# A rewritten order of steps, and 40 unread matmuls in front, in a fused linear-attention and MLP kernel on one core

## The chip, the cores and the metric

One Trainium2 chip, of which the kernel uses one core. The metric is the device time of one execution in microseconds (us). Times are medians over runs. The profile is one further execution, taken by the hardware profiler; its span runs from the first instruction of the program to the last.

## What is computed

For 8 batches of 8 heads (576 tokens, 64 channels each) the reference computes linear attention with a learned feature map, puts the heads of a token side by side (512 channels, 4608 tokens in all), and sends each token through a two-layer network with an ELU between the layers:

```python
def phi(x):
    proj = np.einsum('bhsd,df->bhsf', x, w_phi)                 # 64 -> 128
    proj = proj - np.max(np.abs(proj), axis=-1, keepdims=True)
    return np.concatenate([np.exp(proj), np.exp(-proj)], axis=-1)
q_p, k_p = phi(q), phi(k)
kv  = np.einsum('bhsf,bhsd->bhfd', k_p, v)
num = np.einsum('bhsf,bhfd->bhsd', q_p, kv)
den = np.einsum('bhsf,bhf->bhs', q_p, np.sum(k_p, axis=2))[..., None] + 1e-06
x = (num / den)          # then (4608, 512), heads side by side
h = x @ w_in             # 512 -> 2048
g = np.where(h > 0, h, np.exp(np.minimum(h, 0)) - 1)
out = g @ w_out          # 2048 -> 512
```

All matmuls of the kernel are in bf16 with fp32 accumulation; the output is fp32.

## The kernel before, in words

**Two halves.** The attention half works on 16 groups n of four heads, two groups to a batch. The network half works on 9 chunks of 512 tokens; chunk b consists of tokens of batch b, and the ninth collects the last 64 tokens of each batch. Both halves run interleaved over the whole kernel, so that one half's matmuls fill the time in which the other's elementwise work is under way.

**An order written by hand.** The program is one string, `ORDER`, of 1797 letters. Every letter is one step of a fixed kind with its own list of arguments, and each time a letter occurs it takes the next argument of its list. A star chooses the other engine or form, a digit the PSUM bank that the step begins to fill. Instructions are emitted in the order of the string. Each engine runs its own instructions in that order and waits for the data of others through semaphores. So for each engine the string fixes what stands ahead of what, and nothing else does. PSUM has 8 banks; a step that fills a bank waits until the bank's previous content has been read.

The kinds of step that the prediction uses, with their lines:

- loads on GpSimd's queue: `e`, `f`, `g` (L209: keys, queries, values of a batch, converted to bf16), `h` (L218: the two halves of `w_in`), `i` (L221: `w_out`)
- transposes of keys and queries: for groups 0 to 3 on TensorE, `j`, `l` (L233), with their PSUM copies `k`, `m` (L240); for the other groups by a DMA, `n`, `o` (L254, L259) on SyncE's queue
- keys: `A` (L287, project), `C` (L305, VectorE takes the largest absolute value), `B` (L298, ScalarE takes both exponentials), `D` (L315, the exponential of the maxima), `E` and `F` (L324, L333, GpSimd scales the values), `U` (L509, 36 matmuls each, the key-value product), `V` (L519, its copy)
- queries: `M` (L346, L361), `N` (L374, L388, maxima on VectorE), `O`, `P`, `Q` (L414 to L426, the maxima are split and transposed), `S` (L469, L481), `T` (L493, exponentials on ScalarE), `W` (L542, L558, the product with the key-value matrix), then the division (`X` or `x`, `R`, `y`, L572 to L608), and the transposes of the result, `Y`, `Z` (L623, L633) or the DMA `z` (L649, L656)
- network: `p` (L665, four matmuls, of 512 columns, or of 256 in chunk 0), `q` (L676, exponential on ScalarE), `r` (L681, clamp on GpSimd), `s` (L685, ELU on VectorE), `t` (L693, four matmuls of 512 columns), `u` (L703, copy), `v` (L709, store)
- start: `a` (L174 to L179, the load of `w_phi`, three memsets on VectorE, the identity on GpSimd), `b` (L182, L187, bf16 copies of `w_phi`), `c`, `d` (L192, L201, selector matrices on VectorE)

TensorE works on the whole array (128 rows) in `p`, `t`, `W`, `P`, `Y`, `j`, `l`, and on the upper and the lower 64 rows in turn in `A`, `M`, `S`, `U`. There are 550 TensorE steps of 3914 matmuls in all, each with a weight load of its own.

Of the kernel before, what the change touches and what calls it, by code (L numbers as in the profile page):

```python
# [15 lines left out]


ORDER = """
eeeacj0j5dkk*bA6CA1A3CBBBBDj0kj5kA6CCBBfl0l2BBmmM1NOgDA4BBfl0l7gmm*P1QS2TCDefA0CTM6NOhhgiEEEFFU4
EEUDM2NV*W6XBBP2Q*S4TTM0NM2NFFEU6EEUOP1Qj0j3S4kkM1NV*W6Xl0S2mTTTTl1mY5Z*Y7j6kZOP0W3XQ*S0TTA5Cp2q  # L20
rp7qM3NrssS0TTBp4qA0p3p2CBqrrsj7kl6mqrssM4Np7p3BBM0Np6A4enfDFqrsqrqBrssCp2qp0Y7p3p1rqrZ*O*qrBW6E
sssDqFrl2m*P4Q*p0p5qrXqrEEssM2Np4qrES6TM0NsS2TTTM0NsY6Zp7qrO*sA0A2BBBU4UVCp7qrsp6qrsP5QBt4S0TCp7
qrsp5p6W2XzTW0XDp7EEFqrqrqttA0nS2TTssrsCBp5qrtu*p7p2p3p4t6qrgDBszsqp5qrqS0rstrTsoFsEqp4Tp7rqzS2s
A0rTtEsCToU4qA2BUrzstV*CBW4up7XW0qBt6rXzDBM4FtNzM0M2sA4NvBp7tNqBzrA0sM2O*BCftBENP7t5uQCEDS2M6TtN
FeTS0M6ETtNTEU2S0A6UTCop4VtqTp3rzBsW0qnp4Xrp2qszW0rqu*O*p3DXvBEp5qsvrp7qrszp6rqsFsA0rqM2np4NBEp5
qCrzP3p2rQ*sqp3srqsDp7rqsfp6sqrBp5rsqEsM0qA2p4NBrt7BrsqFS0CgtTsrTS2EM5TNS0toTsTA5U2CTUBS0VvtBW2z
Tt6XTW4uzA0DXS2BtETzCtFETtzBA2M4BS0t7oTCtDTNFtEBvM0A4EM2NBtzNeBU0fu*UA2Cp6Bp5Cqut4rDBsEp7qM2V*r
p6NqEDnW0wstwrqxgM2trNW0FnetxEp5vusS0qM2Rp7syTNp6TFrqS2Rp4qsrTrsp5qsTp7rqysW0qS2xp6rTzrTp4sEzsq
A0U2qCroUrsBp7RV*syA5BCW2p4zxDqW0Eqxp3Brp2rBsRqA0S5qCnt7rTgRtsvTrstBEvsDS3M5TytNzTt2yu*BW3EzS5x
A0tBFzTRM3CtyTNFtzBEwM5S0vU3NTUToA5Vt7BuA0CtCzDtBEW2BtfxBA4p6BRyp3CqDEW0u*wp2qxrBp7FqFsrS0M4TEt6  # L30
NTtrsqtRrsM0ysM3p5NEzp7qNp2rzqsW0rqp4nxrp5qevstrsqsrS0uU2RTUy*S6TzVp4TsW0vqp3xTrp5qoRrsA0qS6p2CT
rp4TsvqsW6qp3rzBrsp5qexBt2rqRS0DA6srotBsytBsyTA3CtETCzW5Dt7FxFBEtBnRM0yA5M3NBztEutNBzEM0wU2CvfUN
DS4V*Et6uW0TvW2xTtxA4M0BntRBW2Nyzp7ECtqt1xFDrup5FsEA2qM6p4NBrp0ECqU6srBUqM2V*tNrA5sS2Bp7swRp4TRC
yqp0TrztqsBtzrqgy*S2u*W5Torp7xDTp1sqS2qRvW5rsTp4rsTp0zyxqW2Fqp7zrsrsA5qvp1gRBxrp4qsBp3rsqyp2Cqrw
zt7sqrsS0EM5sTtnNTrtEDzsS0M3A5TEtCoTt2NFBEA0U3BCURM5Dty*BEVztBNEW3zu*A0S5xBtTt7CTW3RDtxBEA5wM0B
u*FS3ytNBEtTCp2TFuW0qU3xM5rURM0NV*p7yNp4zqsrS5qA0p3sTroCp2Tqsp7qrW4qrsp6DrsBnp3Rqsp2qrvxBt7rzqs
A0S4srBtsBp6y*TCzp3qRp2qrvwtrsqzsDtrTEsvM0A3M5NBp2ENp1qBru*p0qEsvt7qCFrM5p2rsW3NqtrstFsExA0S5Bty
TCt4TRW2By*txzDA0U5BRS2zUyBtEV*zCtuFDEvW0TS5xt7TEzTtu*ETS0U2TFS4UwTtVW0p6xp3qRTRW0rtqyTp2rxp5qs
p4rqRW0rsqp6sursp3yqsp7qrzxp5rqy*zp4qrssW0rzqt6Rrsp3zxp7qy*W0rsqp2xrp5qstrsqtRrsp4systqzRp7rzst5
qtrvsty*tzt7ztvttt4ttp3p2qp1rqstrqsp3rsp2qt1rqsp0rsp3qtrqsp2rsp0qu*p3rqvstrqsup6rvsp5qp3rqsp2rqs  # L40
p6rqstrqst5rsp3p6qp2rqstrqsp3rsp6qutrqvsp7rsp3qp6rqstrqsup7rvst4qutrvstup7vp6qtrqst5rsp7u*p6qvtr
qstrstt7p6p4qtrqsp3rstqtrsp6t4qutruvstvtt7utvttt6tutvtt7u*tvttuv
"""


# [1 line left out]
def kernel(  # L47
# [10 lines left out]
    nc = tc.nc  # L58
# [36 lines left out]
    psum = ctx.enter_context(  # L95
        tc.tile_pool(name="psum", bufs=1, space=bass.MemoryType.PSUM)
    ).tile([P, 8, 512], FP32, name="banks")
# [18 lines left out]
    mhl = [consts.tile([P, 2, D], BF16, name=f"mhl{j}") for j in range(2)]  # L116
# [24 lines left out]

    FIRST = 2
    PLACE_OF = (
        ((0, 1, 5, 6, 2, 3, 4, 7, 8), (0, 1, 4, 5, 2, 3, 6, 7, 8)),
# [189 lines left out]
    def m_mm(n, c, bank=None):  # L336
        if n >= JOINED:
# [32 lines left out]
    def m_max(n, c):  # L370
        if n >= JOINED:
# [357 lines left out]
    def blocks(name, n):  # L729
# [33 lines left out]
        O=(m_split, m_parts),  # L763
# [5 lines left out]
        x=(x_join, x_thirds), R=(x_rec, x_thirds), y=(x_scale, x_thirds),  # L769
# [45 lines left out]
```

## Time and profile before

| | |
|---|---|
| time, median of 3 runs (range) | 366.57 us (366.25 to 367.02) |
| span of the profiled execution | 366.1 us |
| TensorE busy | 347.7 us, 95% of the span |
| VectorE, ScalarE, GpSimd busy | 268.3, 252.5, 212.7 us (73, 69, 58%) |
| first matmul starts, last matmul ends | 4.50 us, about 361.6 us |
| chain that ended last, by engine | TensorE 80%, VectorE 8%, DMA 7%, ScalarE 2%, "issue" 2% |

"Issue" stands for time in which an engine waited for nothing that the profile shows. [...]matmuls overlap in the record: 512 columns have a mean of 380 ns, while a run of four starts one every 216 ns. A busy TensorE is therefore not the same as a TensorE at its peak, and times of steps are read from start to start. The page gives the granted TensorE clock as full in every one of its 40 slices.

### The profile page before, as it was taken

The numbers are of one execution on the slowest core, as the hardware profiler recorded it, in microseconds if no ns is written. First come the engines' busy times: TensorE is split into PE (matmuls) and PEld (weight loads), VectorE is DVE, ScalarE is ACT, GpSimd is POOL, SyncE is SP. The second block draws the span as 40 slices with busy tenths as digits, with TensorE's granted clock in tenths as the row PEclk, the third lists the DMA queues.
The fourth block names the chain that finished last, engine by engine and source line by source line (L and its number), as shares of the span: only waits on it lengthen the run. The fifth ranks groups of instructions, "written<-read, shape, count | busy, mean of one in ns | idle before, by whom it ended". The sixth has DMA issues, their size and how long they took to land.

```text
span 366.1 us, 9813 instructions
## 1 busy us (share of the span) xinstructions
PE 347.7 (95%) x3914; PEld 188.8 (52%) x3914; DVE 268.3 (73%) x474; ACT 252.5 (69%) x481; POOL 212.7 (58%) x323
## 2 busy tenths in 40 slices
PE   2897999999999999999999999999999999999995
PEld 1675676655465444545465445544555444444442
DVE  4887986878976889788979899899858814744300
ACT  4887887878897689876976886888577304554220
POOL 8852857277934878485786497456557504543200
PEclk9999999999999999999999999999999999999999
DMA  7999956699796999965988298053220330213143
GB/s 115 202 213 207 208 82 109 105 159 149 119 144 89 159 135 167 172 96 81 184 165 141 33 181 133 8 109 77 46 48 16 32 75 2 58 29 89 28 98 75
DMA packets 68478, 39.70 MB, mean 108 GB/s; under 512 B 48336, under 2 KB 62800, under 8 KB 68432
## 3 DMA queue, kind: packets, MB, share of 16 engines
q1 hardware_dynamic: 52416, 20.56, 33.3%
q0 software_dynamic: 15856, 18.35, 32.9%
q8 instruction: 30, 0.49, 0.5%
q10 hardware_dynamic: 160, 0.16, 0.1%
q14 instruction: 16, 0.13, 0.1%
HBM read 36.77 MB, written 9.44 MB: 126 GB/s over the span
## 4 chain that ended last, share of the span: by engine, by line
PE 80%; DVE 8%; DMA 7%; ACT 2%; issue 2%; POOL 1%; ACTq 0%; DVEq 0%; POOLq 0%
PE banks L693 32%; PE banks L665 29%; PE banks L509 5%; DMA kn<-in_k_dram 4%; DMA kT<-kn 3%; PE banks L542 3%; PE banks L469 3%; PE banks L287 3%; DVE mk L305 2%; PE banks L558 2%; DVE gT L685 2%; PE banks L346 2%; DVE mq L388 1%; PE banks L361 1%; ACT EK L298 1%
## 5 line engine op out<-in xcount | busy, mean ns | idle before, releaser
L681 POOL TENSOR_SCALAR e_sb<-e_sb 128x512 f32<-128x512 f32 (+1 forms) x160 | 90.9, 574 | 97.0 <-ACT e_sb L676 94.9
L693 PE MATMUL banks<-w_out_sb,gT 128*128 128x512 bf16 x576 | 138.2, 380 | 0.0
L685 DVE SCALAR_TENSOR_TENSOR gT<-e_sb,banks 128x512 bf16<-128x512 f32 (+1 forms) x160 | 96.7, 626 | 44.9 <-POOL e_sb L681 44.5
L676 ACT ACTIVATE e_sb<-banks 128x512 f32<-128x512 f32 (+1 forms) x160 | 87.6, 562 | 60.3 <-PE banks L665 56.9
L665 PE MATMUL banks<-xT,w_in_sb 128*128 128x512 bf16 (+1 forms) x576 | 122.9, 356 | 1.0 <-DVE mq L388 0.9
L665 PEld LDWEIGHTS <-w_in_sb 128*128 128x128 bf16 x640 | 58.8, 98 | 58.6 <-issue 2.7
L298 ACT ACTIVATE EK<-banks 128x768 bf16<-128x768 f32 x96 | 75.3, 814 | 14.6 <-PE banks L287 11.4
L693 PEld LDWEIGHTS <-gT 128*128 128x128 bf16 x576 | 52.5, 98 | 59.8 <-issue 1.9
L324 POOL TENSOR_TENSOR vs<-vn,em 128x576 bf16<-128x576 bf16 x64 | 73.5, 1159 | 15.8 <-ACT em L315 15.7
L493 ACT ACTIVATE Eq<-banks 128x768 bf16<-128x768 f32 (+2 forms) x96 | 73.3, 813 | 9.5 <-PE banks L481 6.1
L305 DVE TENSOR_REDUCE mk<-banks 128x6 f32<-128x768 f32 x48 | 45.3, 951 | 7.9 <-ACT EK L298 3.7
L374 DVE TENSOR_REDUCE mx<-banks 128x6 f32<-128x768 f32 (+1 forms) x30 | 30.7, 1038 | 4.8 <-PE banks L346 3.8
L608 POOL TENSOR_TENSOR xj<-xs,recj 128x448 bf16<-128x448 f32 (+1 forms) x22 | 20.1, 915 | 14.5 <-DVE recj L603 10.6
L703 ACT COPY o_sb<-banks 128x512 f32<-128x512 f32 x23 | 13.3, 590 | 14.5 <-PE banks L693 14.5
L587 DVE TENSOR_TENSOR xs<-banks,e 128x455 f32<-128x455 f32 (+1 forms) x30 | 18.1, 602 | 7.2 <-PE banks L542 5.8
L509 PE MATMUL banks<-vs,EK 64*128 64x65 bf16 x1152 | 23.2, 194 | 0.0
L509 PEld LDWEIGHTS <-EK 64*128 64x128 bf16 x1152 | 21.4, 97 | 2.3 <-issue 1.3
L542 PEld LDWEIGHTS <-Eq 128*128 128x128 bf16 x400 | 16.2, 97 | 7.3 <-issue 1.3
L592 DVE TENSOR_TENSOR xs<-banks,xs 128x455 f32<-128x455 f32 (+1 forms) x30 | 18.3, 609 | 1.1
L287 PE MATMUL banks<-w_sb,kT 64*128 64x128 bf16 x288 | 17.0, 229 | 1.3 <-DMA kT<-kn 0.6
L542 PE MATMUL banks<-kv_sb,Eq 128*128 128x65 bf16 x400 | 17.3, 194 | 0.5 <-DVE kv_sb L519 0.5
L469 PE MATMUL banks<-qT,w_sb 64*128 64x384 bf16 (+2 forms) x102 | 16.3, 324 | 0.9 <-DVE mq L388 0.5
(67 smaller groups left out, 242.2 us busy)
## 6 DMA issues: line engine op xcount, KB each, us to landing
out_dram<-o_sb SPq DMA_DIRECT2D x71, 128.0 KB, 2.5
kn<-in_k_dram POOLq DMA_DIRECT2D x7, 576.0 KB, 9.1
qn<-in_q_dram POOLq DMA_DIRECT2D x7, 576.0 KB, 8.5
vn<-in_v_dram POOLq DMA_DIRECT2D x7, 576.0 KB, 7.4
w_in_sb<-in_moe_w_in_dram POOLq DMA_DIRECT2D x2, 1024.0 KB, 19.6
w_out_sb<-in_moe_w_out_dram POOLq DMA_DIRECT2D x1, 2048.0 KB, 32.3
qn<-in_q_dram POOLq DMA_DIRECT2D x2, 288.0 KB, 7.5
vn<-in_v_dram POOLq DMA_DIRECT2D x2, 288.0 KB, 8.2
```

The lines of the kernel that those rows point to most:

```text
L298: nc.scalar.activation(EK[:, sg, 6 * c:6 * c + 6, :].rearrange("p (i r) f -> p r i f", r=2), st["pk", n, c], ACT.Exp, scale=1.0 - 2.0 * sg,)
L305: nc.vector.tensor_reduce(mk[:, 6 * c:6 * c + 6].rearrange("p (i r) -> p r i", r=2), st["pk", n, c], axis=AX.X, op=ALU.max, apply_absolute ...
L324: nc.gpsimd.tensor_tensor(get(("vs", n), new_vs)[:, sg, r, 0:D], st["v", n // 2][:, 2 * (n % 2) + pr], st["em", n][:, sg, r].unsqueeze(2). ...
L374: nc.vector.tensor_reduce(mq.rearrange("p (v r) -> p r v", r=2)[:, :, v0:v1], st["pm", n, c][:, :, 0:v1 - v0, :], axis=AX.X, op=ALU.max, a ...
L493: nc.scalar.activation(Eq[:, sg, :, :, p0 * D:p1 * D].rearrange("p h r x -> p r h x"), st["pq", n, c][:, :, 0:(p1 - p0) * P].rearrange("p ...
L509: nc.tensor.matmul(kv[:, hi, pr, sg, :], EK[rows, sg, pr * NS + s, :], vs[rows, sg, pr * NS + s, :], start=(s == 0), stop=(s == NS - 1),)
L542: nc.tensor.matmul(pn[:, sg, v - v0, :], Eq[:, sg, hi, par, i0 * D:(i0 + 2) * D], kv_sb[:, hi, pr, sg, :], start=True, stop=True,)
L665: nc.tensor.matmul(ph, w_in_sb[:, ct, jt * P:(jt + 1) * P], xT_of(ch)[:, ct, h0:h1], start=(ct == 0), stop=(ct == N_CT - 1),)
L676: nc.scalar.activation(e_sb, st["ph", ch, jt, h0], ACT.Exp)
L681: nc.gpsimd.tensor_scalar(e_sb, e_sb, 1.0, 0.0, op0=ALU.min, op1=ALU.max)
L685: nc.vector.scalar_tensor_tensor(gT[:, jt, h0:h1], st["e", ch, jt, h0], -1.0, st["ph", ch, jt, h0], op0=ALU.add, op1=ALU.max,)
L693: nc.tensor.matmul(po, st["gT", ch][:, jt, tt * P:(tt + 1) * P], w_out_sb[:, jt, :], start=(jt == 0), stop=(jt == N_JT - 1),)
```

## The change

Two things are changed.

**Unread matmuls.** At the end of `start`, 40 matmuls are emitted ahead of the first transpose. Each multiplies 16 columns of the zeroed tile `mhl[0]` by themselves and writes a corner of PSUM bank 7 that is overwritten before anything reads it. They wait for the first memset alone. They are for the clock of TensorE[...], and they add 80 instructions to its stream.

**The order.** The whole string is replaced. It has the same 1797 letters, and each kind of step still takes its arguments in the same sequence; what differs is how the kinds are interleaved, the bank of 131 TensorE steps, and the engine of some 30 copies and scalings. The new string comes from a search of short moves of steps that also counted the packets in which instructions are fetched. Among the moves:

- at the start the first key projection `A` and its exponential `B` come ahead of `d` and of the second transpose; the second key copy is on VectorE and not on ScalarE; the second half of group 1's key transposes stands behind those of group 0's queries
- `i`, the load of `w_out`, moves from ahead of the first value scalings `E` to behind the first network steps
- later loads are issued earlier (the keys of batch 4, for example, some 40 TensorE steps earlier), and the DMA transposes `n`, `o`, `z` are grouped differently on SyncE's queue
- copies of results (`u`) and stores (`v`) are emitted in groups, and the steps `q`, `r`, `s` of the network in other runs

```diff
 ORDER = """
-eeeacj0j5dkk*bA6CA1A3CBBBBDj0kj5kA6CCBBfl0l2BBmmM1NOgDA4BBfl0l7gmm*P1QS2TCDefA0CTM6NOhhgiEEEFFU4
-EEUDM2NV*W6XBBP2Q*S4TTM0NM2NFFEU6EEUOP1Qj0j3S4kkM1NV*W6Xl0S2mTTTTl1mY5Z*Y7j6kZOP0W3XQ*S0TTA5Cp2q
...
+eeeabcj5kA0Bdj5kA2A4CCBBBj6kA6fl2l0j3CCgmmDM1BBkA4BBDBBfl0NOP3Ql6mm*S2TgCDA0CeTfhhM6NOgEEEFFEEU4
+DFFUV*M2NW6XBBP5Q*M0S4TTM2NNEEU6j1kEEUV*j0k*OP2QS4TTM1NW6Xl0S2l1Y4ZTTj5km*mY7ZOP6Q*W3XS0TTp7A5Cp2
...
+    UNREAD, UNREAD_COLS, UNREAD_BANK = 40, 16, 7
     FIRST = 2
...
         make_identity(nc, ident)
+        zero = mhl[0].rearrange("p r x -> p (r x)")[:, 0:UNREAD_COLS]
+        for _ in range(UNREAD):
+            nc.tensor.matmul(
+                psum[0:UNREAD_COLS, UNREAD_BANK, 0:UNREAD_COLS], zero, zero,
+                start=True, stop=True,
+            )
```

More of the change, by code (lines that the diff above doesn't have):

```diff
@@ L18 @@
 ORDER = """
-eeeacj0j5dkk*bA6CA1A3CBBBBDj0kj5kA6CCBBfl0l2BBmmM1NOgDA4BBfl0l7gmm*P1QS2TCDefA0CTM6NOhhgiEEEFFU4
-EEUDM2NV*W6XBBP2Q*S4TTM0NM2NFFEU6EEUOP1Qj0j3S4kkM1NV*W6Xl0S2mTTTTl1mY5Z*Y7j6kZOP0W3XQ*S0TTA5Cp2q
-rp7qM3NrssS0TTBp4qA0p3p2CBqrrsj7kl6mqrssM4Np7p3BBM0Np6A4enfDFqrsqrqBrssCp2qp0Y7p3p1rqrZ*O*qrBW6E
-sssDqFrl2m*P4Q*p0p5qrXqrEEssM2Np4qrES6TM0NsS2TTTM0NsY6Zp7qrO*sA0A2BBBU4UVCp7qrsp6qrsP5QBt4S0TCp7
-qrsp5p6W2XzTW0XDp7EEFqrqrqttA0nS2TTssrsCBp5qrtu*p7p2p3p4t6qrgDBszsqp5qrqS0rstrTsoFsEqp4Tp7rqzS2s
@@ L24 @@
[L24 to L41, printed above, removed]
@@ L42 @@
-qstrstt7p6p4qtrqsp3rstqtrsp6t4qutruvstvtt7utvttt6tutvtt7u*tvttuv
+eeeabcj5kA0Bdj5kA2A4CCBBBj6kA6fl2l0j3CCgmmDM1BBkA4BBDBBfl0NOP3Ql6mm*S2TgCDA0CeTfhhM6NOgEEEFFEEU4
+DFFUV*M2NW6XBBP5Q*M0S4TTM2NNEU6j1kEEUV*j0k*OP2QS4TTM1NW6Xl0S2l1Y4ZTTj5km*mY7ZOP6Q*W3XS0TTp7A5Cp2
+qrqrM3NS0TTissBp4qrj7kA0p3p2CsBqql6mrsrM4Nsp7p3BBM0Nqqp6p2DqqrrrA4BensssO*Cp0qY7Z*p3qp1qrsrrssrs
+EW6XBl2m*p0p4qM2qrsrP1p5Q*DqES6TNM0NsS2TTTM0NFErsEFY6Zp7qrO*sA0BBA2BU4UVp7qp6CP5Q*qBt4S0Tforrss
+p7qp5CTrsqp6qW2XW0p7ttXDqS2TA0ngrsErsrsEp5p6p7qrtTCp2qFqrrBsp3qqrp5u*BsqssrsrsDFp4qp7qrsErsS0TT
@@ new lines @@
+S2TTt6ttA0zzU4CoEUVA2CBBtuBBW4W0p7t6vzXXzzzzM2NA4DqBenvzftrsM0NM2Np7qrstA0BBBCDM2Ntu*O*P7Q*Ct5S2
+TTtM6S0TTEEFNtM6NEFU3S0ogEUVfA6CtW3TTBBDEp1p0p2XW6Xuqrqqp5qp3p4p7p6srsA0nerrqqrsssqrsBBM2NqO*rr
+p5p4p2qrCsqssDrqp1qp7P3Q*qsp6p5rrssErsFqA2BBM0NCEqp4rrssqrsFt7S0TtS2M5TTTNvvzzzzS0oTTtA5CEU2US0t
+Vu*BBDFETTwW2XW4Xvt6A0BBCS2Ttttu*S0M4TTA2CDTFt7ttM0NBBA4BBM2NNCEEEgfDFEEztU0UV*A2CDzzp6qBup5qrr
+W0xRt4tBp7qEEressoM0M2p6qrtNNW0xp5qsstu*S2M0p7p6TTrsRNqwp4qqrsS2TTyW0xrrssyp5p7qrqrS2TTnnA0CRp6q
+vvzossp4qFU2UV*rsrsBBA5CDzvyzzW2xRp7qp4W0xp3p2rsyBBqrqzqS5TA0nCrrREyzzTssswDBBt7ttS3TTM5NEEEtu*
@@ new lines @@
+t2W3xRyA0BBS5ToTtttuCM3NM0NS5TTFFt7U3UA5A0tV*CCDBBDwBBW3xttuA2Czzp4qp5qfBBW0xEEEep7qrFFrrgssst6t
+M1NS3TTtp7qRRM0NM3Np5p2nevvqrsyW0xqrrssEp3p7p4tS0oqrqqrrsssU2UVy*zzRyvzzuvS5TTTTp4qrW1xRp3qp5qrr
+ssA0CS6TTp2qp4rDqp3W6qErrssxBBp5qrt2S0oA6BnssRByEtA3sttTTyzCDECFFW5xRyzzBBuvt7tM0A4BBM2NNttM0CED
+ENU2UV*wS4TTt6W0W2ttA4nu*vzxxBBM0p7W2tFERqNuCDyxt1p5qA2BBgrsM6Np4qp0wqEECrsU6FfUV*M2NwtRy*A5CS2T
+Tp7rsrRy*qtS2ovtsrsBBDETTgp4qrW5xRyp0uvp7qqS2TTsW5xp1qrp4rssqrrssA5nzzzzW2xRCp0qrp7p1p4p3qqqrrss
+BBqp2qsyzrsErrFt7S0M5NttDFEETTssS0TToA5CM3Ntt2RyA0CBBBBU3UVM5NtzzzuvW3xRDtS5A0nCtFyEW3t7tTTBxRBD
@@ new lines @@
+wA5BBS3TTM0u*Ntp2qCW0xtuM5NFEEyzEU3UVM0NS5TovvrsRp7p3qqrsrsA0CTp4qp2p7qqByrrsp6qp3rqBrrssW4xssp2
+qrst7A0BBS4Tp6p3p2ttqrqCqrrsssRyTDFEM0NA5BBM3NCtDuvp2qrsp1qrFt7EW3xp0qp2RyrqrzzzzEM3S5TTttsNssW3
+xRyA5BBA0BCCwwDEFEEtut2tS3TTDEEU5UttV*Bt3W4S6S0ttxRy*u*TTTTW6xW4Rtt2xS0TTFU6Uy*Vzzp4p1u*qqrrsW5
+p0p7qrssxqrp4p3p1p0qqrqRyssRrrW5xRp7tttsqrszy*y*W3xsp1p5qqrrp6p4p3vzzvqrvzzzzu*vRysszp2zqqrqrrsq
+p7sqsrssrst1tttu*vt5tttt7ttuvp4p2p5p3qrtp0uvsqrqsrsqrqrssp4qp1p7t5tp6p0p2ttqqrrrsssp3p4qrqsrsuqq
+qp7p1qrrrssrssp5qrqp2p0qp7rsrqrssp4sqrst1tttuqrst7tttt0tttuvu*vp1qp5p2rqrqrsssp4p7qrsqp1p2p0p5qq
@@ L43 @@
+rrqsst7tttuqp1p7qp3rsrqsqrst4ttrrrssstvu*vvt0tttt7ttu*tut6vvvtttuv
 """
```

## The prediction

> **What bounds the kernel now.** I read the page first, for the engines, then a table by stage (the stages cut where TensorE's state changes), then TensorE's waits, then the timeline of the first 60 us, and last the chain.
>
> ```profile
> PE 347.7 (95%) x3914; PEld 188.8 (52%) x3914; DVE 268.3 (73%) x474; ACT 252.5 (69%) x481; POOL 212.7 (58%) x323
> ```
>
> ```profile
> 4.50:20.00 15.50, 11.96 (x179) 9.20 (x180) 12.23 (x21) 12.20 (x25) 13.67 (x20) 1.00 1.17 189
> 20.00:28.60 8.60, 6.70 (x174) 5.31 (x174) 7.04 (x15) 7.19 (x12) 3.70 (x7) 1.00 1.13 213
> 28.60:48.00 19.40, 16.89 (x267) 12.99 (x268) 17.80 (x39) 16.89 (x40) 12.39 (x24) 1.00 1.20 203
> 48.00:100.00 52.00, 51.99 (x686) 30.54 (x679) 41.48 (x76) 41.55 (x83) 33.16 (x58) 1.00 0.75 119
> 100.00:150.00 50.00, 49.13 (x636) 25.88 (x635) 41.01 (x70) 41.74 (x79) 33.58 (x47) 1.00 1.11 140
> 200.00:250.00 50.00, 49.50 (x588) 25.50 (x586) 45.30 (x79) 41.08 (x78) 31.17 (x44) 1.00 0.51 85
> ```
>
> A row of the table has the stage, its length, then busy time of TensorE, its weight loads, VectorE, ScalarE and GpSimd, clock, DMA share and GB/s. From 48 us on TensorE has no idle time to speak of; before that it is idle 3.5, 1.9 and 2.5 us in three stages, after 4.5 us in which it has no data. In the third VectorE is busy 17.80 of 19.40 us, 92%.
>
> A busy TensorE may still run below its peak. So I took, for each kind of step, the median distance from its start to the next step's start after 60 us: 863 ns for the 144 `t` and the 128 `p` of 512 columns, 434 for the 32 half `p`, 577 for the 32 `U`, 168 for the 48 `A`, 439 and 378 for the 30 `W` of groups 6 to 15, and so on (the steps that occur early alone were set by column count from these). Their sum over 550 steps is 320.7 us. To this comes a cost of changing between full rows and half rows:
>
> ```profile
> 98.34 0.86 PE banks L693 x4
> 99.64 0.97 PE banks L693 x4
> ```
>
> The same four matmuls take 0.86 us on the chain when full-row work follows, 0.97 when a half-row step follows. Over all kinds a change, either way, costs 97 ns in the step ahead of it and 11 in the one behind, 108 in all; 158 changes make 17.1 us. TensorE's floor is 320.7 + 17.1 = 337.8 us. The span is then 4.5 (first data) + 337.8 + 19.1 (all that runs slower than the floor) + 4.7 (last matmul to last store). The 19.1 by place, from the step starts: 9.6 up to 20.3 us, 2.4 from there to 28.6, 3.8 to 48, and 3.3 in all the rest.
>
> **First stage: a slow clock, and waits.**
>
> ```profile
> 14.12 1.17 PE L233 MATMUL banks<-ident,qn 128*128 128x128 bf16 x9
> 23.86 0.67 PE L233 MATMUL banks<-ident,kn 128*128 128x128 bf16 x9
> 28.54 0.22 PE L623 MATMUL banks<-ident,xp 128*128 128x128 bf16 x1 [1.21 <-issue]
> ```
>
> Nine transposes take 1.17 us at 14.12 and 0.67 at 23.86: (1.17 - 0.26) / 8 = 114 ns apart against (0.67 - 0.22) / 8 = 56. The 72 `U` matmuls of group 0 take 2.00 us on the chain, later ones 1.15. So the array runs at half speed until about 19.5 us, though the page's clock row says full.
>
> **Second: instructions.** At 27.3 us TensorE stops for 1.21 us for "issue". The queue table has 30 packets of instructions, 0.49 MB, on one queue[...]. By the queue table of short windows one of the 30 falls between 26 and 27 us, none between 21.3 and 26, while the loads keep the DMA engines at 107% and more.
>
> **Third: VectorE.**
>
> ```profile
> PE banks L665 <- DVE mq L388: 0.9, 1, 0.9
> PE banks L469 <- DVE mq L388: 0.5, 1, 0.5
> PE banks L361 <- DVE mq L388: 0.4, 1, 0.4
> ```
>
> [...]
>
> **The change, part by part.**
>
> *Unread matmuls.* The trace has none of 16 columns. The nearest full-row row is `W`, 65 columns: 40 in 1.25 us at 52.70, 31 ns each; at half clock 62. So 40 take 1.2 to 2.5 us. They can start after the first memset, at about 1.0 us, and end at 2.2 to 3.5, before the first keys land at 4.50. Cost: nothing, hidden by that load. Their gain is the question. They fill 16 x 40 = 640 columns, at half clock 0.5 us of array time, while the stage from 4.5 to 17 us, where TensorE is recorded busy for over half of the time, left the clock low. I take it that they don't raise it: gain 0. If they did, the slow part of the chain shrinks: `U` of group 0 by 0.85, projections, selection matmuls and a transpose block ahead of it by about 1.0, together 1.9 us.
>
> *Start order.* `B` of group 0 no longer stands behind a ScalarE copy and the second transpose: with the first three blocks transposed at 5.1, a copy of 0.35 and six matmuls of 0.5, ScalarE's exponentials start at about 6.1 instead of 7.57, 1.4 us ahead. On GpSimd `i` leaves the front of the scalings:
>
> ```profile
> 12.21 1.15 POOL L221 DMA_DIRECT2D w_out_sb<-in_moe_w_out_dram  x1 [0.71 <-DMA vn<-in_v_dram]
> 13.37 3.38 POOL L324 TENSOR_TENSOR vs<-vn,em 128x576 bf16<-128x576 bf16 x3
> ```
>
> The values land at 12.21, so the first `E` can start 1.15 us sooner. But the first `U` also stands behind `S` of group 0, and that behind the query maximum `N` (13.91 to 15.15 us), which waits for queries that land at about 10.7; in the new order five more transposes stand between. So both leads mostly end as slack: -0.2 us. `i` is now issued at about 32 us; the loads ahead of it last until about 33.6 (values of batch 1 land 23.8 us after their issue at 10.76) and it needs some 10 us at 200 GB/s, so `w_out` lands near 45, ahead of the first `t` (49.82). Cost 0.
>
> *Packets.* 80 more instructions put every crossing 40 matmuls earlier. In the old order the packet that ran out at 27.1 us had been begun some 128 matmuls before, at 22; now it begins at about 20.5 and still has both `U` of group 1 in it, some 5 us of work[...]. The stall may thus stay, at `W` of group 1. I take -0.5, bounds 0 and -1.4.
>
> *28 to 48 us.* The work put ahead of `U` of group 2 on VectorE, counted from the second `Y`, falls from 20.9 to 20.5 us (durations of before, old and new string): 0.4. VectorE's idle share is 8%, 1.6 us; half-chunk `p` steps stand further ahead of their readers, so part of it closes. I take -0.9, bounds 0 and -2.
>
> *After 48 us.* The floor falls by 0.2 (156 changes for 158). The keys of batch 4 are issued 24 us of TensorE work earlier, which ends the 0.6 us wait of group 8's `A` for its transposed keys. The wait for a `kv_sb` copy (0.5) at group 12 is left with a shorter lead. Against that `W` of group 7 now stands only 0.26 us of TensorE work behind its `U`, whose copy takes 0.59: +0.5. What else there is above the floor after 48 us, 3.3 less these two waits, some 2 us in pieces of 0.1 to 0.3, is rearranged; I take a fourth of it off. Sum: -0.6 + 0.5 - 0.5 - 0.2 = -0.8. The 64 last matmuls, copies and stores keep their shape: 0.
>
> Sum: -0.2 - 0.5 - 0.9 - 0.8 = -2.4 us from 366.57: 364.2.
>
> **The rivals.**
>
> - *The clock does rise early.* For: nothing else would use TensorE before 4.5 us, and half the excess lies ahead of 20 us. Against: 0.5 us of array time. 364.2 - 1.9 = 362.3.
> - *VectorE takes it all back.* It sets the pace from 28.6 to 48, its sum hardly changes, and what is won ahead of it becomes its slack. 366.4: no change.
> - *Slower.* Ahead of the `p` of chunk 2 the new string puts 3 to 5 us more VectorE work than the old (121.9 against 116.6 us ahead of jt 12), where VectorE is 82% busy; with the kept stall, +0.5 at group 7, and a like wait at group 12, TensorE waits some 2 us more after 100 us. 368.2.
>
> **How the numbers follow.** My forecast 0.50, the early clock 0.22, no change 0.12, slower 0.16. Its two unknown terms (0 to -1.4 for 0.5, 0 to -2 for 0.9) put it between 362.2 and 365.6. The range reaches to the early clock with a part of those below, 361.5, and just past no change above, 366.8; the slower case is left out. Faster by over 0.2% (0.7 us): 0.50 + 0.22 and a part of the third, 0.75. Within: 0.09. Slower: 0.16.
>
> **What would show it.** Nine transposes near 14 us in 1.17 us again: the clock; in 0.67, the first rival. The start of `U` of group 0 near 17.4; the "issue" wait of TensorE gone, or at `W` of group 1; VectorE above 92% from 28 to 47; `U` of group 2 at about 46 instead of 47.61; no wait for `kT` after 100 us, one of 0.5 for `kv_sb` at group 7. Wrong it would be if TensorE were idle over 1 us between 100 and 250.

## The result, and the profile after

| | before | after |
|---|---|---|
| time, median (range) | 366.41 us (366.25 to 367.02) | 364.92 us (364.18 to 370.93) |
| ratio after / before, 95% interval | | 0.9949 (0.9927 to 0.9972) |
| span of the profiled execution | 366.1 us | 363.4 us |
| TensorE, VectorE busy | 347.7, 268.3 us | 345.4, 269.9 us |

The change is faster by 0.5%. A second measurement of the same kernel (e5 below) gave 365.54 us, 0.996 (0.9934 to 0.9985). Some executions of most kernels here are several us longer than the rest; medians are over all of them, ratios leave out those over 1.5% above the kernel's fastest. The profiled run of before took 367.91 us with all overheads, 1.3 us above that kernel's usual time, so the two profiles differ by more (2.7 us) than the medians do (1.5).

The engines' row of the page after, and the table by stage (stage, length, busy time of TensorE, weight loads, VectorE, ScalarE, GpSimd, clock, DMA share, GB/s):

```profile
PE 345.4 (95%) x3954; PEld 187.0 (51%) x3954; DVE 269.9 (74%) x474; ACT 251.2 (69%) x480; POOL 211.4 (58%) x324
```

```profile
4.50:20.00 15.50, 10.94 (x196) 7.99 (x197) 13.90 (x25) 12.93 (x27) 13.75 (x20) 1.00 1.16 186
20.00:28.60 8.60, 8.26 (x205) 6.67 (x204) 6.94 (x16) 6.98 (x12) 2.46 (x6) 1.00 1.12 213
28.60:48.00 19.40, 16.74 (x281) 12.89 (x276) 18.58 (x39) 18.44 (x43) 13.57 (x25) 1.00 1.12 178
48.00:100.00 52.00, 51.27 (x643) 29.45 (x641) 41.65 (x73) 41.08 (x84) 35.43 (x60) 1.00 1.04 158
100.00:150.00 50.00, 49.54 (x666) 26.20 (x666) 42.44 (x70) 42.12 (x79) 32.21 (x44) 1.00 0.74 115
```

TensorE does 17 matmuls more in the first stage (196 for 179) and 31 more in the second (205 for 174), where its idle time falls from 1.90 to 0.34 us. In the third it is idle as long as before (2.66 for 2.51 us), and VectorE is busy 18.58 of 19.40 us, 96%.

TensorE's timeline after (start, length in us, operation, count, and in brackets the idle time ahead with what ended it):

```profile
0.99 1.16 PE L183 MATMUL banks<-mhl 128*16 128x16 bf16 x40 [0.99 <-DVE mhl L178]
4.55 0.50 PE L240 MATMUL banks<-ident,kn 128*128 128x128 bf16 x3 [2.41 <-DMA kn<-in_k_dram]
13.02 0.71 PE L240 MATMUL banks<-ident,qn 128*128 128x128 bf16 x5
14.57 0.39 PE L240 MATMUL banks<-ident,qn 128*128 128x128 bf16 x4
16.41 1.33 PE L516 MATMUL banks<-vs,EK 64*128 64x65 bf16 x72
23.92 0.23 PE L368 MATMUL banks<-w_sb,qT 64*128 64x128 bf16 x2 [0.24 <-issue]
```

The 40 unread matmuls take 1.16 us and have ended 2.4 us before the first keys. Five transposes at 13.02 are still slow, (0.71 - 0.26) / 4 = 112 ns apart, four at 14.57 run at full speed, (0.39 - 0.22) / 3 = 57 ns, and `U` of group 0 takes 1.33 us where it took 2.19. A stop for instructions of 0.24 us is left, in an `M` just ahead of `W` of group 1 (24.09 us); the one of 1.21 us in `Y` is gone.

TensorE's waits after, those that answer to the ones of before and the two that are new:

```profile
PE banks L672 <- DMA xT<-xj: 1.2, 1, 1.2
PE banks L672 <- DVE mq L395: 0.9, 1, 0.9
PE banks L353 <- DMA qT<-qn: 0.7, 1, 0.7
PE banks L476 <- DVE mq L395: 0.5, 1, 0.5
PE banks L368 <- DVE mq L395: 0.4, 1, 0.4
```

The three waits for VectorE (`mq`) between 28 and 48 us are what they were, to a tenth. Two waits for transposes by DMA have come: `p` of chunk 3 for `xT`, 1.2 us at 156.39, and `M` of group 6 for `qT`, 0.7 us at 88.42. Those of before for `kT` at group 8 (0.6) and for `kv_sb` at group 12 (0.5) are gone. The chain of waits around the first of them (start, length, what):

```profile
145.19 1.21 SPq L261
...
146.45 1.27 SPq L261
...
147.81 8.54 DMA xT<-xj
...
156.39 1.24 PE banks L672 x5
```

Two transposes of queries (L261) now stand on SyncE's queue ahead of the one of `xT`, which lands 8.54 us after its issue.

Set against the same floor (sum of the steps at their usual pace, 337.55 us for the new order, 337.77 for the old), the time above it is, by place:

| up to | before | after | difference |
|---|---|---|---|
| `W` of group 0, first step (20.27, 18.82 us) | 9.61 | 7.89 | -1.72 |
| `W` of group 0, second (28.92, 26.55 us) | 2.38 | 1.25 | -1.13 |
| `U` of group 2 (47.61, 45.47 us) | 3.77 | 3.78 | 0 |
| the end of TensorE's work | 3.38 | 3.66 | +0.28 |

Between these two profiles the whole gain lies in the first 29 us; what comes later gives a little back. Not all of it need be the change. The profiled run of before was a long one, and e12 below, whose order is that of before in the first 70 us, comes to `U` of group 2 at 46.07 us, with 8.52 and 1.67 us in the first two rows.

### The profile page after: what moved, and what is told of

Read it like the earlier page. It is cut to its first block, busy times and chain, and to the rows that moved or that the text cites. A ratio compares the mean times of both kernels' runs of the same rounds, so it can differ in the third digit from the quotient of the medians.

```text
span 363.4 us, 9891 instructions
## 1 busy us (share of the span) xinstructions
PE 345.4 (95%) x3954; PEld 187.0 (51%) x3954; DVE 269.9 (74%) x474; ACT 251.2 (69%) x480; POOL 211.4 (58%) x324
## 4 chain that ended last, share of the span: by engine, by line
PE 77%; ACT 7%; DVE 7%; DMA 6%; issue 1%; SPq 1%; POOL 0%; ACTq 0%; DVEq 0%; POOLq 0%
PE banks L700 32%; PE banks L672 27%; PE banks L516 4%; PE banks L549 3%; ACT EK L305 3%; DMA qT<-qn 3%; PE banks L476 3%; DMA xT<-xj 2%; PE banks L294 2%; DVE gT L692 2%; ACT Eq L500 2%; PE banks L353 2%; DVE mq L395 2%; PE banks L565 1%; ACT e_sb L683 1%
## 5 line engine op out<-in xcount | busy, mean ns | idle before, releaser
L688 POOL TENSOR_SCALAR e_sb<-e_sb 128x512 f32<-128x512 f32 (+1 forms) x160 | 89.7, 570 | 92.8 <-ACT e_sb L683 88.7
L700 PE MATMUL banks<-w_out_sb,gT 128*128 128x512 bf16 x576 | 136.0, 380 | 0.2 <-DVE gT L692 0.2
L672 PE MATMUL banks<-xT,w_in_sb 128*128 128x512 bf16 (+1 forms) x576 | 121.5, 356 | 2.1 <-DMA xT<-xj 1.2
L692 DVE SCALAR_TENSOR_TENSOR gT<-e_sb,banks 128x512 bf16<-128x512 f32 (+1 forms) x160 | 94.7, 626 | 35.4 <-POOL e_sb L688 34.9
L305 ACT ACTIVATE EK<-banks 128x768 bf16<-128x768 f32 x96 | 73.4, 814 | 13.5 <-PE banks L294 8.6
L710 ACT COPY o_sb<-banks 128x512 f32<-128x512 f32 x21 | 12.4, 590 | 34.5 <-PE banks L700 32.1
L615 POOL TENSOR_TENSOR xj<-xs,recj 128x448 bf16<-128x448 f32 (+1 forms) x23 | 20.5, 892 | 13.3 <-DVE recj L610 13.3
L516 PE MATMUL banks<-vs,EK 64*128 64x65 bf16 x1152 | 21.5, 191 | 0.1
L516 PEld LDWEIGHTS <-EK 64*128 64x128 bf16 x1152 | 20.0, 94 | 2.3 <-DVE mx L381 0.8
L710 DVE COPY o_sb<-banks 128x512 f32<-128x512 f32 x15 | 10.3, 685 | 11.1 <-PE banks L700 11.1
```

The source lines that it names most:

```text
L305: nc.scalar.activation(EK[:, sg, 6 * c:6 * c + 6, :].rearrange("p (i r) f -> p r i f", r=2), st["pk", n, c], ACT.Exp, scale=1.0 - 2.0 * sg,)
L516: nc.tensor.matmul(kv[:, hi, pr, sg, :], EK[rows, sg, pr * NS + s, :], vs[rows, sg, pr * NS + s, :], start=(s == 0), stop=(s == NS - 1),)
L672: nc.tensor.matmul(ph, w_in_sb[:, ct, jt * P:(jt + 1) * P], xT_of(ch)[:, ct, h0:h1], start=(ct == 0), stop=(ct == N_CT - 1),)
L688: nc.gpsimd.tensor_scalar(e_sb, e_sb, 1.0, 0.0, op0=ALU.min, op1=ALU.max)
L692: nc.vector.scalar_tensor_tensor(gT[:, jt, h0:h1], st["e", ch, jt, h0], -1.0, st["ph", ch, jt, h0], op0=ALU.add, op1=ALU.max,)
L700: nc.tensor.matmul(po, st["gT", ch][:, jt, tt * P:(tt + 1) * P], w_out_sb[:, jt, :], start=(jt == 0), stop=(jt == N_JT - 1),)
```

## The experiments

**The theory after the two profiles**: the unread matmuls matter only as instructions, by moving the place where TensorE needs its next packet of instructions, and the rest of the gain is the order's. DMA queue q8 has 30 packets of instructions before and 31 after, 0.49 and 0.51 MB. If it serves TensorE alone, 7828 and 7908 matmuls and weight loads make 261 and 255 to a packet; from these I estimate 256, or 128 matmuls with their loads. **Rivals**: the unread matmuls raise the clock earlier; they do nothing; or, for the order, that the gain lies in one half of it alone.

### How many unread matmuls, and with which order

```diff
# e1: the new order without them; e2: with 128
-    UNREAD, UNREAD_COLS, UNREAD_BANK = 40, 16, 7
+    UNREAD, UNREAD_COLS, UNREAD_BANK = 0, 16, 7
# e3 and e4: the old order with 40 and with 128
+        zero = mhl[0].rearrange("p r x -> p (r x)")[:, 0:UNREAD_COLS]
+        for _ in range(UNREAD):
+            nc.tensor.matmul(
...
```

> The new order without the 40 unread matmuls. In the changed kernel transposes went from 107 ns apart at 10.7 us to 56 ns at 14.6, in the kernel before only at about 19.5. Theory clock: the unread matmuls brought that forward; without them U of group 0 takes 2.0 us again (1.15 to 1.33 with them), the clock rises at about 18 to 19 us, and the time is 0.8 to 1.5 us above the changed kernel's 364.7. Theory order: the clock rises by 14.6 us all the same because the new order keeps TensorE at work from 10.7 to 13.7 without a pause; time 364.7. Theory packets: every crossing falls 40 matmuls later, and the wait for instructions near 24 us changes from 0.2 us to over 1, at a place about 40 matmuls further on; time 365.5 to 366.

> The new order with 128 unread matmuls, 256 instructions or one whole packet more than none, so that packets fall as in the new order without any. 128 x 25 ns last 3.2 us, from 1.0 to 4.2, still ahead of the first keys at 4.55. Theory clock: the array is already at full speed at the first transposes or soon after (56 ns apart at 8.2 us), and the time is 0.3 to 1 us below that of 40. Theory order: as the new order without unread matmuls, within 0.3 us. Theory packets: an equal wait for instructions as the new order without unread matmuls, at the same matmuls.

> The kernel before with the 40 unread matmuls alone. Theory clock: the slow part ends at about 14 us instead of 19.5, U of group 0 takes 1.2 instead of 2.0 us, and 1 to 1.5 us are gained: 365.0 to 365.5. Theory order: the clock rises at 19.5 as before, no gain from it. Theory packets: the wait of 1.21 us for instructions at 27.3 us moves 40 matmuls ahead, to W of group 1 near 25 us, and changes its length; the time moves by up to 1 us either way.

> The kernel before with 128 unread matmuls: crossings of packets at the same matmuls as before, the clock alone is changed. Theory clock: full speed from about 5 to 8 us on; 1.5 to 2 us gained up to U of group 0, of which the wait for instructions at 27.3 us may take some back because TensorE comes to it earlier; 364.8 to 365.6. Theory order: nothing, 366.4.

Measured, against 366.56 us for before in the same session:

| | order | unread | median (range), us | ratio, interval | first instruction packets at, us |
|---|---|---|---|---|---|
| before | old | 0 | 366.56 | 1 | 20.2, 26.2, 32.2 |
| e1 | new | 0 | 367.57 (365.32 to 373.07) | 1.0011 (0.9988 to 1.0035) | 19.0, 24.9, 30.7 |
| after | new | 40 | (above) | 0.9949 (0.9927 to 0.9972) | 14.3, 21.6, 27.5 |
| e2 | new | 128 | 366.79 (365.90 to 376.53) | 1.0000 (0.9975 to 1.0025) | 4.8, 19.3, 25.2 |
| e3 | old | 40 | 369.91 (365.87 to 373.93) | 1.0047 (1.0019 to 1.0074) | 14.2, 22.2, 28.1 |
| e4 | old | 128 | 366.56 (365.71 to 370.45) | 0.9997 (0.9965 to 1.0029) | 4.5, 19.7, 25.7 |

The new order alone is worth nothing that can be measured. 40 unread matmuls make it faster, and 128 of them don't. 128 is, by the estimate above, just one packet: one more comes at 4.5 to 4.8 us, and the others come where they come without any. 40 move them all to other places. So neither the activity nor the number alone sets the time; where the packets fall fits it.

The stops for instructions show the packets themselves. I counted TensorE's matmuls, unread ones included, ahead of each stop in the first 30 us: 351 in before, after and e1 (and in e9 and e12 below), 479 in e2 and e4, 223 and 351 in e11. These places lie 128 matmuls apart, whatever the order. The stops add up to 0.50 to 1.78 us in the six profiled kernels with no unread matmuls or 128, and to 0 to 0.45 us in the eight with 40.

TensorE's timeline of e4, with 128:

```profile
0.99 3.36 PE L183 MATMUL banks<-mhl 128*16 128x16 bf16 x128 [0.99 <-DVE mhl L178]
14.00 1.17 PE L240 MATMUL banks<-ident,qn 128*128 128x128 bf16 x9
17.27 2.19 PE L516 MATMUL banks<-vs,EK 64*128 64x65 bf16 x72
27.96 0.22 PE L630 MATMUL banks<-ident,xp 128*128 128x128 bf16 x1 [0.78 <-issue]
```

3.36 us of them, right up to the first keys, leave the array at half speed at 14 us and in `U` at 17.27: 9 transposes in 1.17 us, 72 matmuls in 2.19, as in before. The stop for instructions is in the same `Y` again, and shorter than in before, 0.78 us for 1.21. So 3.36 us of this activity don't bring the clock up; whether 40 matmuls, placed as they are, have a part in it is a question for e5 to e8. In e3, with 40, the same `Y` runs through, on TensorE's timeline:

```profile
26.13 0.86 PE L630 MATMUL banks<-ident,xp 128*128 128x128 bf16 x8
```

And yet e3 is slower than before. TensorE's timeline of its profiled run, which took 372.45 us and so is one of the longer ones, and of before at the same place:

```profile
137.31 0.50 PE L294 MATMUL banks<-w_sb,kT 64*128 64x128 bf16 x6 [4.54 <-DMA kT<-kn]
137.61 2.19 PE L516 MATMUL banks<-vs,EK 64*128 64x65 bf16 x72
```

```profile
134.81 0.34 PE L287 MATMUL banks<-w_sb,kT 64*128 64x128 bf16 x6 [0.57 <-DMA kT<-kn]
134.99 1.31 PE L509 MATMUL banks<-vs,EK 64*128 64x65 bf16 x72
```

TensorE comes to group 8 about 1.5 us earlier in e3, and its keys land 2.5 us later. After 4.54 us of waiting the array is back at half speed: the next `U` takes 2.19 us for 1.31. This is one way in which the old order can lose what was won early, but being early is not enough for it. The profile of e6 below has the old rest too, TensorE comes to group 8 almost as early, and it finds its keys there:

```profile
133.21 0.34 PE L294 MATMUL banks<-w_sb,kT 64*128 64x128 bf16 x6
```

What differs is the transposes of these keys. SyncE's queue is at the two of them for 9.21 us in e3 and for 8.10 in before, but for 4.07 in e4 and 4.93 in e6, from about the same start (121.5 to 122.8 us). Why, no run here shows. The new rest has more room: in after the keys are loaded at 83.9 us and not at 113.6 to 115.1, and their transposes begin at 113.3.

### The changed kernel again, and the two halves of the order

e5 is the changed kernel again. e6 and e7 have 40 unread matmuls and change the order at `V` of group 2 (some 50 us): e6 the new start and the old rest, e7 the old start and the new rest.

```diff
# e6, at the seam
-ErsEFY6Zp7qrO*sA0BBA2BU4UVp7qp6CP5Q*qBt4S0Tforrssp7qp5
+ErsEFY6Zp7qrO*sA0BBA2BU4UVfCp7qrsp6qrsP5QBt4S0TCp7qr
...
# e7, at the seam
-TTM0NsY6Zp7qrO*sA0A2BBBU4UVCp7qrsp6qrsP5QBt4S0TCp7qrs
+TTM0NsY6Zp7qrO*sA0A2BBBU4UVp7qp6CP5Q*qBt4S0Torrssp7qp5C
...
```

> The changed kernel itself once more, beside the runs below. Four kernels had TensorE's clock rise at 19 to 20 us, the changed kernel's first trace at about 14. If that was chance, the rise is at 19 to 20 here, U of group 0 takes 2.0 us, U of group 2 starts near 46.2 instead of 45.47, and the time is 365 to 365.5. If the order brings it about with just 40 unread matmuls, it is at 14 again and the time is 364.7. The wait for instructions: 0.2 to 0.4 us before W of group 1, as in the first trace.

> 40 unread matmuls, the new order up to the copy V of group 2, and from there the remaining steps in the old order. Theory start (all of the gain is made before 48 us, the rest gives a little back): U of group 2 at 45.5 to 46.3 and the time as the changed kernel's or up to 0.5 us below it. Theory loads (the old rest issues its loads too late for a TensorE that comes 1.5 to 2 us earlier): A of group 8 waits for its transposed keys for 2 us or more instead of 0.6, and the time is 366 to 369, as it was for the old order with 40 unread matmuls.

> 40 unread matmuls, the old order up to V of group 2, then the new one. Theory start: U of group 2 at about 45.9 to 46.3, as the old order with 40 unread matmuls had it; the new rest adds its wait of 1.4 us or more for xT ahead of chunk 3; time 365 to 366. Theory loads: no wait for kT at group 8, so the time is 1 to 3 us below that of the new start with the old rest.

| 40 unread matmuls | median (range), us | ratio to before, interval |
|---|---|---|
| e5, new start, new rest | 365.54 (364.08 to 370.58) | 0.9960 (0.9934 to 0.9985) |
| e6, new start, old rest | 371.31 (366.19 to 377.43) | 1.0011 (0.9973 to 1.0050) |
| e7, old start, new rest | 364.49 (363.69 to 365.11) | 0.9925 (0.9897 to 0.9953) |
| e3, old start, old rest | 369.91 (365.87 to 373.93) | 1.0047 (1.0019 to 1.0074) |

The new start is worth nothing that these times show (e7 is not slower than e5), and the gain needs the new rest: e3 loses it clearly against e7. e6's interval still touches that of e5, but half of its runs took over 372 us. e6's profile is of one of its shorter runs (366.48 us) and shows no long wait, nor the one of over 2 us for `kT` that the theory of the loads had forecast; so what makes most of its runs longer isn't shown.

e5 was also to tell whether the early clock of after was chance. TensorE's matmuls are the same up to some 48 us in after, e5, e6 and e8 (below). `U` of group 0 in e5, then in e8:

```profile
16.40 1.33 PE L516 MATMUL banks<-vs,EK 64*128 64x65 bf16 x72
```

```profile
16.76 2.19 PE L516 MATMUL banks<-vs,EK 64*128 64x65 bf16 x72
```

In e5 it takes 1.33 us as in after, in e6 and e8 2.19. With the old start and 40 unread matmuls it takes 1.66 us in e7, 1.73 in e9, 1.65 in e10 and 2.19 in e3. With none or 128 it takes 1.62 in e11 and 2.16 to 2.19 in before, e1, e2, e4 and e12. So full speed comes at different times in runs with the same matmuls, and once early without unread ones. It comes early in five of eight profiles with 40 and in one of six others: too few to say whether the 40 help it. The rival of the early clock is thus not excluded for 40. The stop for instructions is gone in e5, e6 and e8.

### The transpose that `p` of chunk 3 waits for

e8 is the changed kernel with one letter moved: the transpose `o` of the queries of group 10 goes behind those of the network's next chunk.

```diff
-A0BBS5ToTtttuCM3NM0NS5TT
+A0BBS5TTtttuCM3NM0NS5TT
...
-BDwBBW3xttuA2Czzp4qp5qf
+BDwBBW3xttuA2Czzop4qp5qf
```

> The changed kernel with one step moved: the DMA transpose o of group 10's queries now stands behind the two z that fill chunk 3's xT, instead of ahead of them. In the changed kernel the second p of chunk 3 waited 1.38 us because the last xT took 8.5 us from issue to landing behind two qT transposes. Theory queue: the wait falls to under 0.3 us, M of group 10 (some 5 us of TensorE work later) does not wait, and the time is 1.0 to 1.4 us below the changed kernel in the same call. Theory loads: xT is late because the DMA engines are busy with other transfers, and the wait stays within 0.4 us of what it was.

364.80 us (363.18 to 369.27), 0.9937 (0.9907 to 0.9968), an interval that overlaps e5's, so the time alone decides nothing. The profile does: SyncE's queue in e8 has the two `xT` ahead of the `qT`,

```profile
151.86 1.20 SPq L656 DMA_TRANSPOSE xT<-xj  x1
153.12 1.22 SPq L663 DMA_TRANSPOSE xT_last<-xj  x1
154.44 2.80 SPq L261 DMA_TRANSPOSE qT<-qn  x2
```

and TensorE's waits after 130 us no longer have `xT`. That one profiled run has another wait, earlier, which no edit of mine touched. TensorE's timeline of e8:

```profile
70.55 1.03 PE L700 MATMUL banks<-w_out_sb,gT 128*128 128x512 bf16 x4
71.50 0.34 PE L294 MATMUL banks<-w_sb,kT 64*128 64x128 bf16 x6
75.27 0.50 PE L368 MATMUL banks<-w_sb,qT 64*128 64x128 bf16 x6 [3.42 <-DMA qT<-qn]
76.10 1.49 PE L700 MATMUL banks<-w_out_sb,gT 128*128 128x512 bf16 x3 [0.33 <-issue]
```

3.42 us for `qT` of group 5, and three `t` matmuls in 1.49 us after it (the record of the fourth is missing) where four took 1.03 before: at half speed again. The same step doesn't wait so in after or e5. The three profiled runs far above their kernel's shortest (e2, e3, e8) each have one wait of 3.4 to 5.1 us after 48 us, of three different steps. In the other profiles, e10 and e12 aside, the longest is 2.2 us. So such waits seem to make the longer runs; one profile per run can't prove it.

### Both together, the packets once more, and loads moved alone

```diff
# e9: e7 with the move of e8
-BDwBBW3xttuA2Czzp4qp5qf
+BDwBBW3xttuA2Czzop4qp5qf
...
# e11: e7 without unread matmuls
-    UNREAD, UNREAD_COLS, UNREAD_BANK = 40, 16, 7
+    UNREAD, UNREAD_COLS, UNREAD_BANK = 0, 16, 7
# e10 (with 40 unread) and e12 (without): the old order, five e moved, of batches 3 to 7.
# batch 4, taken from
-FtEBvM0A4EM2NBtzNeBU0fu*UA2Cp6Bp5Cqu
+FtEBvM0A4EM2NBtzNBU0fu*UA2Cp6Bp5Cqu
# and put to
-qrszp6rqsFsA0rqM2np4NBEp5qCrzP3p2r
+qrszp6rqsFsA0rqM2enp4NBEp5qCrzP3p2r
# batch 7, put to (20 TensorE steps ahead of its old place)
-qtRrsM0ysM3p5NEzp7qNp2rzqsW0rqp4nx
+qtRrsM0ysM3p5NEzp7eqNp2rzqsW0rqp4nx
...
```

> Both best edits together: 40 unread matmuls, the old order up to the copy V of group 2 and the new order after it (364.49 alone), and the transpose of the queries of group 10 issued behind that of the network's chunk 3 (which took away the 0.9 us that the first p of chunk 3 waits in that kernel). Theory (the waits are separate and add): 363.6 us, the first p of chunk 3 waits less than 0.3 us. Rival (TensorE that comes earlier meets the next late transfer, as the query transposes of group 5 did once): 364.5 us or more, with a wait of over 1 us for qT or kT elsewhere.

> The old order with 40 unread matmuls (369.91 us alone, with a wait of 4.6 us for kT at A of group 8) and one thing of the new order: the loads e of the keys of batches 3 to 7 are issued as early as there (batch 4 about 40 TensorE steps earlier, the others 5 to 20). Nothing else differs. Theory (the old order loses because the keys of batch 4 are loaded too late for a TensorE that comes earlier): no wait of over 0.3 us for kT at group 8, and 364.8 to 365.6 us, that is 4 to 5 us below the same order with late loads. Rival (the rest of the new order matters as a whole, some other late transfer takes the wait): 368 us or more, with a wait of over 1 us for a DMA at another place.

> The old order up to V of group 2 and the new order after it, without unread matmuls (with 40 of them 364.49 us). Theory (unread matmuls act through the place at which TensorE needs its next instruction packet): the issue wait of 1.2 us before the transposes of group 0's result is there again near 27 us, and U of group 2 starts near 47.4 us and not at 45.3; 365.6 to 366.2 us. Rival (they do nothing with an order whose rest has its loads in time): 364.5 us.

> The kernel before with one change: the loads e of the keys of batches 3 to 7 are issued as early as in the new order, no unread matmuls. Theory (two causes that need each other: loads in time only pay their full worth once TensorE is earlier): only the wait of 0.6 us for kT at group 8 goes, 366.0 us, ratio 0.998 to 0.999. Rival (the loads alone are the gain of the change): 365.0 us or less.

| | median (range), us | ratio to before (366.58 us), interval |
|---|---|---|
| e9, e7 and e8 together | 363.61 (363.31 to 364.12) | 0.9886 (0.9848 to 0.9923) |
| e10, old order, key loads early, 40 unread | 373.55 (373.19 to 375.26) | 1.0163 (1.0122 to 1.0203) |
| e11, old start, new rest, no unread | 367.02 (364.69 to 371.24) | 1.0005 (0.9986 to 1.0024) |
| e12, old order, key loads early, no unread | 376.08 (374.56 to 377.12) | 1.0220 (1.0178 to 1.0262) |

**e9** beats both kernels: its interval lies wholly below those of after and of e5, measured in other sessions. It overlaps those of e7 and e8, so that the two edits add is likely and not shown by the times. `p` of chunk 3 runs through on its timeline, eight matmuls in one piece, while in e7, shown second, the last five have waited for `xT`:

```profile
154.67 1.90 PE L672 MATMUL banks<-xT,w_in_sb 128*128 128x512 bf16 x8
```

```profile
154.93 1.24 PE L672 MATMUL banks<-xT,w_in_sb 128*128 128x512 bf16 x5 [0.74 <-DMA xT<-xj]
```

**e11** is 1 us slower than expected, and shows the packets at their plainest. Its timeline of TensorE has two stops for instructions:

```profile
21.28 0.25 PE L516 MATMUL banks<-vs,EK 64*128 64x65 bf16 x5
22.11 1.25 PE L516 MATMUL banks<-vs,EK 64*128 64x65 bf16 x67 [0.58 <-issue]
...
28.04 0.22 PE L630 MATMUL banks<-ident,xp 128*128 128x128 bf16 x1 [1.20 <-issue]
```

0.58 + 1.20 = 1.78 us. In e7, the same order with 40 unread matmuls, neither is there; in the place of the first, `U` waits 0.27 us for its scaled values. Between `W` of group 0 (19.23 us in e11, 18.90 in e7) and `U` of group 2 (47.12, 45.34) e7 gains 1.45 us, which is about 1.78 - 0.27; the spans differ by 1.9. The clock has no part in this pair: `U` of group 0 takes 1.62 us in e11 and 1.66 in e7. But 1.45 is the far end of what the profiles show. From `W` of group 0 to `U` of group 2 the old start takes 26.00 to 26.65 us with 40 unread matmuls (e3, e7, e9, e10) and 26.64 to 27.89 without or with 128 (before, e4, e11, e12); the new start 26.42 to 26.65 (after, e5, e6, e8) and 26.99 to 27.07 (e1, e2). In both stops TensorE goes on about the same time after its packet starts: 22.11 - 19.65 = 2.5 us and 28.04 - 25.78 = 2.3. So it does in before (28.54 - 26.20 = 2.3) and in after (23.92 - 21.59 = 2.3).

**e10 and e12** miss by 8 and 10 us. Up to `t` of chunk 2 e10 did what I expected: no wait for `kT` at group 8, and that `t` at 139.16 us, level with after (139.26) and 2.4 us ahead of before (141.60). Then GpSimd, TensorE and VectorE stop together. Their timelines in e10, GpSimd, then VectorE, then TensorE:

```profile
163.24 1.15 POOL L331 TENSOR_TENSOR vs<-vn,em 128x576 bf16<-128x576 bf16 x1
169.62 0.83 POOL L216 DMA_DIRECT2D kn<-in_k_dram  x1 [5.23 <-DMA kT<-kn]
170.47 2.35 POOL L688 TENSOR_SCALAR e_sb<-e_sb 128x512 f32<-128x512 f32 x4
```

```profile
171.13 0.69 DVE L692 SCALAR_TENSOR_TENSOR gT<-e_sb,banks 128x512 bf16<-128x512 f32 x1 [6.13 <-POOL e_sb L688]
```

```profile
171.88 1.87 PE L672 MATMUL banks<-xT,w_in_sb 128*128 128x512 bf16 x4 [4.74 <-DVE gT L692]
```

A load `e` writes a tile of keys that must first have been transposed out. Moved ahead of the last transpose of the keys that its tile still held, it waits 5.23 us for it on GpSimd; the clamps `r` (L688) stand behind it in GpSimd's order, the ELU `s` (L692) waits for them 6.13 us, and `p` for the bank that the ELU reads, 4.74 us. e12 has the same wait on GpSimd, 6.3 us. So this edit does not give the new order's gain. Nor does it settle whether earlier loads would: the load that waits is that of batch 7, which the edit put ahead of the last transpose `n` of batch 5 (group 11), whose tile it takes. The new order has the load behind that `n`. Batch 4 moved alone wasn't tried.

## Why the prediction was right, point by point

The total was right, 364.2 us against 364.92, but in good part by luck: two of its four terms, -1.7 of the -2.4 us, did not come, and the early part gave more than I had counted, some of it from a profile of before that was a long run. By the stages above:

- **Unread matmuls: 0 for the clock.** Right for 128 (e2, e4), open for 40. In the profile after the clock does rise near 14.5 us, which was my mark for the rival, and so it does in e5; but in e8, with the same matmuls up to there, four transposes take 0.63 us at 14.62 and `U` 2.19: there it rises at about 19.5. So the mark was a poor one. By the first `W` the early rise is worth 8.67 - 7.89 = 0.8 us. With the same matmuls the rise thus varies by some 5 us from run to run; I had not reckoned with that, and no run here shows what sets its time.
- **Start order: -0.2.** Measured -1.72 in the two profiles, of which 0.8 is that clock. The rest is not the order's for certain: at the first `W` the profiled runs of the old start have 7.91 to 9.61 us above the floor (e7 lowest, before and e4 highest), those of the new start 7.88 to 8.67. The ranges overlap, and e7 against e5 shows no gain in the time. So -0.2 is neither confirmed nor refuted. One difference is seen: in the old start the nine transposes of group 1's keys begin anywhere from 7.93 to 9.29 us, and in five of eight profiles they wait for the load, up to 1.48 us; in the new start they don't wait.
- **Packets: -0.5.** Of about the right size for the new start: from the first `W` to `U` of group 2 after, e5, e6 and e8 take 0.3 to 0.7 us less than e1 and e2. The -1.13 of the stage has the 1.21 us stop of before in it, where e12, with the same start, stopped for 0.52. The pair e7 and e11 gives -1.45, about the far bound (-1.4). What I had mis-sized is the time from the matmul 128 ahead of the stop to the end of the stop: I took 6.4 us, an estimate from the two times 22.1 and 28.5 in before; it is 5.9 in before (22.61 to 28.54) and 5.0 in after (18.96 to 23.92). And that matmul came at 19.0 us, not at 20.5. To count from there was my choice, and no trace shows that a packet's time begins at that matmul: on q8 the packet starts at 26.20 us in before and 21.59 in after, 2.3 us ahead of the end of the stop. The stop did move to `W` of group 1, as I had said it might, with 0.24 us.
- **28 to 48 us: -0.9.** Wrong, 0 above the floor. From the second `W` of group 0 to `U` of group 2 takes 18.68 to 18.71 us in all eight profiles with the old start and 18.91 to 18.93 in all six with the new one, however early TensorE comes to it. So VectorE took nothing back, as the second rival would have it, and gave nothing. The step that failed is the 0.4 us less of VectorE work, summed from durations of before: counted from the second `Y`, VectorE is busy 18.77 us for 18.07. Of these 0.70 us 0.62 are one instruction of `O` (L422), 0.80 us for 0.18; why it is longer isn't shown. VectorE did close up, from 92 to 96%, but over more work, and TensorE's three waits for it stayed 0.9, 0.5 and 0.4 us.
- **After 48 us: -0.8.** Wrong by about 0.9: +0.28 above a floor that fell by 0.22. Two of the named parts came: the `kT` wait went, and so did the `kv_sb` wait of group 12, which I had left standing. The forecast wait of `W` of group 7 for `kv_sb` doesn't show as such: TensorE is idle 0.42 us just ahead, at an `A` whose bank an ELU still reads, and the copy ends meanwhile. What I had not seen is SyncE's queue: the wait of 1.2 us for `xT` comes from the way in which `o` and `z` are grouped there, which I had listed and not followed; for the 0.7 us for `qT` no run tested it. The fourth that I took off the small waits had no working behind it.
- **"Wrong if TensorE were idle over 1 us between 100 and 250."** It was, 1.2 us for `xT`, and the total held all the same, because the first 29 us gave more than I had counted.

What the prediction didn't see at all is that the parts need each other. With 40 unread matmuls the old rest keeps no gain (e3, 1.0047; e6, 1.0011), and the new rest without the packets' gain is level with before (e1, 1.0011; e11, 1.0005). Why the old rest loses it is only partly settled: in e3's profile it is the wait at group 8, which e6's has not. And which moves of the new rest matter is open: the loads of keys moved as a set make a worse wait, and no run moved the others one at a time.

## What to carry to other kernels

Time won early can be lost again at any later transfer that lands just before its reader (4.54 us for `kT` in e3); look, before you count a gain at the start, at how far ahead of its reader each later transfer lands, and in more than one run. An earlier load is not free either: in an engine's queue it blocks everything behind it until its tile is free (5.23 us on GpSimd in e10), so move it up to the last reader of that tile and no further. And in a kernel bound by its instruction stream for a moment, a few idle instructions can move that moment to a place where it is shorter or hidden (0.24 us in after for 1.21 in before); try several counts, since one packet's worth (128 matmuls here) left the later stops in place (0.58 us in e2, 0.78 in e4). Last, sum an engine's work from the profile after as well: one instruction that takes 0.6 us longer than before undid the 0.4 us of less work forecast here.

## What was unexpected in the hardware

- 128 matmuls of 16 columns take 3.36 us and 40 take 1.16, so 2.20 us for 88: 25 ns each, although nine transposes at 14.00 us of the same run (e4) still go at half speed. The prediction took 31 to 62, from a row of 65 columns.
- TensorE's array went back to half speed after one wait of 3.42 us (e8, three `t` matmuls in 1.49 us) and after one of 4.54 (e3, `U` in 2.19); after the 1.2 us of after and one of 2.18 us in e1 the next five `p` matmuls take 1.24 us, at full speed.
- With the same matmuls on TensorE up to 48 us, the clock rises near 14.5 us in two runs (after, e5; four transposes in 0.39 us, `U` of group 0 in 1.33) and at about 19.5 in two others (e6, e8; `U` in 2.19).
- With the loads' packets (q0) at 107 to 112% of the 16 DMA engines in the microseconds around four of the packets of instructions (26.20 in before, 21.59 in after, 19.65 and 25.78 in e11), TensorE stops for instructions at places 128 matmuls apart, and goes on 2.2 to 2.5 us after the packet starts, in nine stops of eight profiled runs.
